# Gated mix of attention and SwiGLU: half of the input turned on TensorE, the last output tiles paced and the feed-forward part added by an identity product

## Chip, cores and metric

The kernel runs on one core of one Trainium2 chip. The metric is the device time of an execution in microseconds. A second number appears beside it, the span of the profiled execution: the time from the profile's first instruction to its end, which is a little shorter than the device time of the same execution. Engine names are those of the profile: PE (TensorE), PEld (its weight loads), DVE (VectorE), ACT (ScalarE), POOL (GpSimd), SP (SyncE).

## What is computed

```python
def _A_ref(x, wqkv, wo):                 # attention, S = 2048, D = 512, H = 32, Dh = 16
    qkv = (x @ wqkv).reshape(B, S, 3, H, Dh).transpose(2, 0, 3, 1, 4)
    q, k, v = qkv[0], qkv[1], qkv[2]
    scores = jnp.einsum("bhqd,bhkd->bhqk", q, k) * (Dh ** -0.5)
    p = softmax(scores, axis=-1)
    o = jnp.einsum("bhqk,bhkd->bhqd", p, v)
    return o.transpose(0, 2, 1, 3).reshape(B, S, D) @ wo

def _B_ref(x, w_gate, w_up, w_down):     # feed-forward, F = 1792
    return (silu(x @ w_gate) * (x @ w_up)) @ w_down

g = sigmoid((x * gate_w).sum(-1, keepdims=True))
out = g * _A_ref(x, wqkv, wo) + (1 - g) * _B_ref(x, w_gate, w_up, w_down)
```

All inputs and the output are bf16. Both halves read the same x (2048 tokens by 512).

## The kernel before

**Tiling.** Queries go in four blocks of 512 (`qb`), heads in eight groups of four (`g`); a pair of the two is a unit, 32 units in all. A unit runs over 16 tiles of 128 keys. For each key tile the scores of four heads are needed, in two pairs: two products on PE write a `s_t` tile of 128 x 1024, and one activation on ACT turns it into `e_t` (exp). Part of the key tiles goes another way: their scores land in `d_t`, and DVE makes the exponential from integer and fp16 arithmetic in `y_t` (with `z_t`, `u_t`, and free parts of `kaug` or `wd_t` as scratch). Value products (`o_ps`) gather both kinds into one bank; the softmax's sums come with them, from a column of ones in `vaug`.

**Order.** The work of PE, DVE and ACT is put in a fixed order when the program is built, by a small planner with a clock for each engine (`Plan`, costs in microseconds). `Pacer` holds side work in chains of pieces with a release and a due slot: the projections of Q, K and V, the gate, the feed-forward products (`gu_chain`, `down_pieces`) and the output products (`fin_pieces`). Where a pair of banks is filled together, `two_banks` lets two products of half height run side by side in the array. `m_tile` hands out three PSUM banks (m0 to m2) in turn; a further pool gives the two score tiles, tag `s`, and one bank holds the value products, tag `o`. `keep_warm` puts products on zeros into PE's queue. The planner also puts value products with zero weights (`o_ps<-xT`) where it sees PE idle.

**The head.** x is needed with its columns on the partitions (`xT`). Nine transposing loads on SP's queue bring it, the first four for tokens 0 to 1023 and the rest for the other half. Behind them on the same queue stand the plain loads of the remaining weights. On ACT's queue stand three small loads: 64 columns each of the K, Q and V weights, for head group 0. DVE copies the first two, spaced out, into `wpad`. PE then makes K of group 0 for all tokens (`k0`, into `kp0`), Q for the first block (`qp0`) and V (`v0`). `largest` takes the greatest magnitude of K per partition, `kneg` is the bound derived from it, `bp0` its product with |Q|, and the last step of DVE folds it into the query `q0[0]`. Then the first scores can go out. `ones_rows` fills rows of `kaug` with ones; groups 1 to 4 on DVE, 5 to 7 on POOL.

**The gate.** g is made as 0.5 (1 + tanh(z/2)), in `gval`, and 1 - g in `omg`, once for all tokens.

**The tail.** The feed-forward result of a block is scaled by `omg` when it leaves PSUM (`down_pieces`, into `bblk`). For the last block, `tail(0)` puts eleven output products ahead of the last value products and `tail(1)` one behind them; `last_mm` adds the products of the last two head groups, and `store` makes gval times PSUM plus `bblk` on DVE, tile by tile, and sends each tile from SP's queue.

Of the kernel before, what the change touches and what calls it, by code (L numbers as in the profile page):

```python
# [9 lines left out]
ALU = mybir.AluOpType  # L10
# [68 lines left out]
def kernel(  # L79
# [89 lines left out]


    xT = big.tile([P, DC, S], BF16, name="xT")
    parts = [(0, 2 * QBW, dc) for dc in range(DC)] + [(2 * QBW, S, dc) for dc in range(DC - 1)]
    parts += [(2 * QBW, 3 * QBW, DC - 1), (3 * QBW, S, DC - 1)]
    for t0, t1, dc in parts:
        nc.sync.dma_start_transpose(out=xT[:, dc, t0:t1], in_=x[t0:t1, dc * P:(dc + 1) * P])
    wqk = big.tile([P, DC, 2 * D], BF16, name="wqk")
    for c0 in (D, 0):

        nc.scalar.dma_start(out=wqk[:, :, c0:c0 + 64],
                            in_=A_wqkv[:, c0:c0 + 64].rearrange("(dc p) c -> p dc c", p=P))  # L180

    rb = big.tile([P, NB, QBW], BF16, name="rb")
    wv = rb[:, :, :]
# [7 lines left out]
    wo_t = big.tile([P, NB, D], BF16, name="wo_t")  # L191

    wo_l = big.tile([P, 2, D], BF16, name="wo_l")
    wd_t = big.tile([P, FC, D], BF16, name="wd_t")

    def late_loads():
        nc.sync.dma_start(out=gw_col[:], in_=gate_w.rearrange("(dc p) -> p dc", p=P))
# [35 lines left out]
    def ones_rows(engine, g):  # L233

        engine.memset(kaug[:, g, :].bitcast(F32), 1.0019378662109375)
    for g in range(1, 4):
        ones_rows(nc.vector, g)
    vaug = big.tile([P, KT, G * 4 * VC + 16], BF16, name="vaug")
    nc.gpsimd.memset(vaug[:, :, G * 4 * VC:], 0.0)

# [23 lines left out]
    ident = const.tile([P, P], BF16, name="ident")  # L264
    nc.gpsimd.memset(ident[:], 1.0)
    nc.gpsimd.affine_select(out=ident[:], in_=ident[:], pattern=[[-1, P]], compare_op=ALU.is_equal,
                            fill=0.0, base=0, channel_multiplier=1)

    kb = const.tile([P, NB], F32, name="kb")
    kneg = const.tile([P, NB, 8], BF16, name="kneg")  # L270
# [108 lines left out]
    def two_banks(n, name, a, b, end):  # L379

        st = {}

        def pc(k):
            v, i = divmod(k, n)

            def f():
                if k == 0:
                    while m_ready(2) is None:
                        stuck()
                    st["a"], st["b"] = m_tile(name + "_a"), m_tile(name + "_b")  # L390
                if k == n:
                    sync(ordered(nc.tensor.nop()), st["half"])
                    spend("R", 0.1 if st["seq"] < plan.seq else 1.5)
                for ps, (w, r), h in ((st["a"], a(i), v), (st["b"], b(i), 1 - v)):
                    rows = slice(64 * h, 64 * h + 64)
                    st["half"] = mm(ps[:, :], lhsT=w[rows, :], rhs=r[rows, :], start=(k == i == 0),
                                    stop=(k == 2 * n - 1), tile_position=(64 * h, 0), skip_group_check=True)
# [195 lines left out]
    def gate_pieces(t0):  # L593
        def f():
            gp = m_tile("glog")
            for t in (t0, t0 + 1):
                for dc in range(DC):
                    mm(gp[:, t:t + 1], lhsT=xT[:, dc, t * P:(t + 1) * P],
                       rhs=gw_col[:, dc:dc + 1], start=(dc == 0), stop=(dc == DC - 1))
            spend("F", 2)  # L600

            def end():
                vec.tensor_copy(out=ge[:, t0:t0 + 2], in_=gp[:, t0:t0 + 2])
                m_free(gp, plan.dve)
            later(0.15, end)
        return [(0.7, f, True)]

    def gate_end():
        act(out=ge[:, :], in_=ge[:, :], func=ACT.Tanh, scale=0.5)
        plan.act += 0.2  # L610

        def end():
            vec.tensor_scalar(out=gval[:, :], in0=ge[:, :], scalar1=1.0, scalar2=0.5, op0=ALU.add, op1=ALU.mult)
            vec.tensor_scalar(out=omg[:, :], in0=ge[:, :], scalar1=-0.5, scalar2=0.5, op0=ALU.mult, op1=ALU.add)
        later(0.4, end, plan.act + 0.2)


    def gu_chain(qb, fc):
# [28 lines left out]
            later(0.6, gated, plan.act + 0.25, (qb, fc))  # L647
        return load, two_banks(DC, "gu", rows("g"), rows("u"), done_gu)

    def down_pieces(qb, tq):  # L650

        def rows(t):
            return lambda fc: (mt[:, fc, t * P:(t + 1) * P], wd_t[:, fc, :])

        def done_down(pa, pb):
            for t, p in ((tq, pa), (tq + 1, pb)):
                later(0.65, lambda t=t, p=p: end(t, p))

        def end(t, p):
            n = qb * TQ + t  # L660
            vec.tensor_scalar(out=bblk[:, t, :], in0=p[:, 0:D], scalar1=omg[:, n:n + 1],
                              scalar2=None, op0=ALU.mult)
            m_free(p, plan.dve)
        return two_banks(FC, "dps", rows(tq), rows(tq + 1), done_down)

# [246 lines left out]
    def store(t, a_ps, base, o_t=None):  # L912
# [3 lines left out]
                                 op0=ALU.mult, op1=ALU.add)  # L916
        nc.sync.dma_start(out=out_f[t * P:(t + 1) * P, :], in_=o_t)

    def fin_pieces(qb, tq):
# [40 lines left out]
    for dc in range(DC):  # L960
# [3 lines left out]
        if dc < DC - 1:  # L964
            keep_warm(2)
# [6 lines left out]
    k0_evict(0)  # L972
    for dc in range(DC):
        if dc < DC - 1:
            for tb in (2, 3):
                k0(dc, tb)
        if dc == 0:
            v0(0)
        elif dc < DC - 1:
            keep_warm(3)  # L980
    ones_rows(vec, 4)
    k0(DC - 1, 2)
    largest(1, kp0[1][:, 0:QBW])
    vec.scalar_tensor_tensor(out=kneg0, in0=bsel0, scalar=kpart0[:, 1:2], in1=kneg1, op0=ALU.mult, op1=ALU.min)
    k0(DC - 1, 3)
    largest(2, kp0[1][:, QBW:2 * QBW])
    vec.scalar_tensor_tensor(out=kneg0, in0=bsel0, scalar=kpart0[:, 2:3], in1=kneg0, op0=ALU.mult, op1=ALU.min)
    k0_evict(1)
    v0(8)
    bp0 = m_tile("bp0")  # L990
# [67 lines left out]
    for qb in range(QB):  # L1058
# [37 lines left out]
    def finish(un):  # L1096
# [6 lines left out]
        if un == UNITS - 2:  # L1103
            here[un] = recip_here(osbs[un])
            spend("F", 1, plan.dve + 0.2)
            for i in range(TQ):
                def part(cs=slice(i * P, (i + 1) * P)):
# [2 lines left out]
                                      op=ALU.mult)  # L1110
                    if cs.stop == QBW:
                        m_free(here[un][0], plan.dve)
                later(1.2, part)

    def close(un):
# [80 lines left out]
            pace.cur = c  # L1196
        pace.credit -= emit_piece(c)

    a_ps = []

    def last_mm(w, on):
        for tq in range(TQ):
            mm(a_ps[tq][:, 0:D], lhsT=on[:, tq * P:(tq + 1) * P], rhs=wo_l[:, w, :], start=False, stop=(w == 1))

    def tail(k):

        if k == 0:
            assert all((QB - 1, b) in normed for b in range(NB - 1))
            a_ps.extend(m_tile("a_l")[:, :] for _ in range(2))
            al = ps_s.tile([P, 2 * QBW], F32, tag="s", name="al")  # L1210
            a_ps.extend([al[:, 0:QBW], al[:, QBW:2 * QBW]])
        todo = [(tq, b) for tq in range(TQ) for b in range(NB - 1)]
        for tq, b in todo[:11] if k == 0 else todo[11:]:
            mm(a_ps[tq][:, 0:D], lhsT=onc[QB - 1][:, b, tq * P:(tq + 1) * P], rhs=wo_t[:, b, :],
               start=(b == 0), stop=False)

    def next_pv():
        flush_act()
        while not pv_list(None):
# [133 lines left out]
    un = UNITS - 1  # L1353
    osb = osbs[un]
    tail(1)
    last_mm(0, osbs[un - 1])
# [47 lines left out]
```

## Time and profile before

| what | us |
|---|---|
| median of 7 runs | 848.31 (847.0 to 848.97) |
| the profiled execution | 847.54 |
| its span | 845.8 |
| first exponential on ACT starts | 18.41 |
| last exponential on ACT ends | 833.94 |
| transposing loads on SP's queue, issue of nine | 0.81 to 13.02 |
| PE's granted clock over the span | 0.994 |

Times within the execution count from the start of the span. A group of the profile names the written and the read tile (out<-in), the shapes, the number of instructions, their busy time and mean, and the idle time of the engine just before them with what ended it. Matmuls overlap in the array: one of 512 columns is shown with about 0.38 us, while a row of them starts every 0.215 us. An engine's idle time costs only where something later waits for it.

### The profile page before, as it was taken

What the parts mean: (1) busy time and instruction counts of PE and PEld (TensorE: products, weight loads), DVE (VectorE), ACT (ScalarE), POOL (GpSimd) and SP (SyncE); (2) the same over time, 40 slices, a digit from 0 to 9 for tenths busy, and PEclk for the clock granted to TensorE, in tenths of its full rate; (3) what the DMA queues carried; (4) which work ended last, traced back from release to release, by engine and by line L of the source; (5) the groups of instructions that cost most, each with busy time, mean ns of one, the idle gap of its engine ahead of it and who ended that gap; (6) DMA issues with size and microseconds to landing.
All of it is one profiled execution on the core that took longest, in us unless ns stands there. A gap on an engine that the chain in (4) does not pass through costs nothing.

```text
span 845.8 us, 16257 instructions
## 1 busy us (share of the span) xinstructions
PE 769.6 (91%) x6078; PEld 263.2 (31%) x6078; DVE 797.2 (94%) x1160; ACT 813.8 (96%) x910; POOL 93.3 (11%) x122
## 2 busy tenths in 40 slices
PE   7999998999889998889899989898999899989996
PEld 3222233332322333222223323223333233233332
DVE  6999998999999999999999899999998999999995
ACT  3999999999999999999999999999999999999994
POOL 5010100010011011011101000101010110110100
PEclk9999999999999999999999999999999999999999
DMA  9432435345454334554443354544532544553331
GB/s 201 130 70 44 89 75 113 69 94 103 95 112 100 65 78 101 104 113 92 96 102 71 78 116 86 110 94 92 106 71 55 112 105 92 109 104 76 74 66 36
DMA packets 101447, 78.23 MB, mean 92 GB/s; under 512 B 77792, under 2 KB 89656, under 8 KB 101368
## 3 DMA queue, kind: packets, MB, share of 16 engines
q0 software_dynamic: 12672, 46.14, 28.7%
q1 hardware_dynamic: 87112, 30.86, 15.4%
q8 instruction: 47, 0.77, 0.4%
q10 hardware_dynamic: 1584, 0.20, 0.2%
q14 instruction: 32, 0.26, 0.1%
HBM read 20.83 MB, written 2.34 MB: 27 GB/s over the span
## 4 chain that ended last, share of the span: by engine, by line
DVE 27%; PE 14%; ACT 8%; issue 3%; DMA 1%; ACTq 0%; DVEq 0%
DVE y_t L166 10%; ACT e_t L160 7%; DVE kaug L166 5%; PE s_t L157 4%; DVE u_t L166 4%; PE o_ps L157 2%; DVE z_t L166 2%; DVE mt L166 2%; DVE gs L166 2%; PE dps_b L157 2%; PE d_t L157 1%; PE dps_a L157 1%; PE gu_b L157 1%; DVE osb L166 1%; ACT th L160 1%
## 5 line engine op out<-in xcount | busy, mean ns | idle before, releaser
L160 ACT ACTIVATE e_t<-s_t 128x1024 bf16<-128x1024 f32 x846 | 792.1, 1106 | 7.7 <-PE s_t L157 5.6
L157 PE MATMUL s_t<-qx,kaug 64*128 64x512 bf16 x1376 | 292.5, 381 | 35.5 <-ACT e_t L160 30.6
L166 DVE TENSOR_SCALAR y_t<-d_t 128x512 uint16<-128x512 f32 x356 | 234.7, 682 | 16.4 <-PE d_t L157 13.7
L157 PEld LDWEIGHTS <-kaug 64*128 64x128 bf16 x2048 | 137.2, 93 | 325.8 <-issue 290.7
L157 PE MATMUL o_ps<-e_t,vaug 128*32 128x512 bf16 x1692 | 160.2, 389 | 2.1 <-DVE osb L166 1.0
L157 PE MATMUL gu_a<-xT,wg 64*128 64x512 bf16 x448 | 136.4, 379 | 0.0
L157 PE MATMUL gu_b<-xT,wu 64*128 64x512 bf16 x448 | 135.0, 378 | 1.2 <-DVE y_t L166 0.9
L157 PE MATMUL d_t<-qx,kaug 64*128 64x512 bf16 x288 | 107.7, 379 | 15.3 <-DVE y_t L166 8.3
L157 PEld LDWEIGHTS <-vaug 128*32 128x32 bf16 (+1 forms) x2148 | 45.9, 93 | 146.8 <-issue 145.5
L772 POOL DMA_DIRECT2D y_t<-u_t x44 | 40.3, 915 | 350.7 <-PE s_t L157 187.8
L772 POOL DMA_DIRECT2D y_t<-kaug x38 | 35.9, 946 | 310.4 <-PE s_t L157 184.5
L157 PE MATMUL dps_b<-wd_t,mt 64*128 64x512 bf16 x224 | 65.0, 375 | 0.3 <-DVE y_t L166 0.2
L157 PE MATMUL dps_a<-wd_t,mt 64*128 64x512 bf16 x224 | 64.9, 376 | 0.0
L166 DVE TENSOR_SCALAR z_t<-y_t 128x2048 uint16<-128x2048 uint16 x89 | 61.5, 691 | 2.1
L166 DVE TENSOR_SCALAR y_t<-y_t 128x2048 uint16<-128x2048 uint16 x89 | 60.9, 684 | 0.8 <-DMA y_t<-u_t 0.4
L166 DVE TENSOR_TENSOR u_t<-u_t 128x2048 f16<-128x2048 f16 x44 | 53.8, 1223 | 1.1
L166 DVE TENSOR_TENSOR u_t<-u_t,z_t 128x2048 f16<-128x2048 f16 x44 | 53.5, 1216 | 0.1
L157 PE MATMUL s_t<-q,kaug 64*128 64x512 bf16 x212 | 44.0, 387 | 7.6 <-ACT e_t L160 7.0
L166 DVE TENSOR_TENSOR kaug<-kaug 128x2048 f16<-128x2048 f16 x39 | 47.7, 1223 | 0.9
L157 PEld LDWEIGHTS <-wg 64*128 64x128 bf16 x448 | 41.5, 94 | 20.7 <-issue 9.0
L166 DVE TENSOR_TENSOR kaug<-kaug,z_t 128x2048 f16<-128x2048 f16 x39 | 47.5, 1217 | 0.1
L157 PEld LDWEIGHTS <-wu 64*128 64x128 bf16 x448 | 42.1, 94 | 15.3 <-issue 0.2
(119 smaller groups left out, 632.2 us busy)
## 6 DMA issues: line engine op xcount, KB each, us to landing
y_t<-u_t POOLq DMA_DIRECT2D x44, 512.0 KB, 4.8
y_t<-kaug POOLq DMA_DIRECT2D x38, 512.0 KB, 5.0
wg<-in_B_w_gate_dram SPq DMA_DIRECT2D x56, 128.0 KB
wu<-in_B_w_up_dram SPq DMA_DIRECT2D x56, 128.0 KB
y_t<-wd_t POOLq DMA_DIRECT2D x6, 512.0 KB, 4.6
on<-osb SPq DMA_DIRECT2D x120, 16.0 KB
rb<-rr SPq DMA_DIRECT2D x15, 128.0 KB
wd_t<-in_B_w_down_dram SPq DMA_DIRECT2D x7, 256.0 KB
```

The source lines that it names most:

```text
L157: return ordered(nc.tensor.matmul(*args, **kw))
L160: ordered(nc.scalar.activation(*args, **kw))
L166: return lambda *a, **kw: ordered(f(*a, **kw))
L772: nc.gpsimd.dma_start(out=ya, in_=ua, accum_op=ALU.add)
```

## The change

Four parts.

1. Only tokens 0 to 1023 of x come by transposing loads. The other 1024 tokens come as two plain loads of 512 KB on ACT's queue, into the still unused tile `wd_t`, one behind the K weights and one behind the Q weights. `turn` multiplies each 128 x 128 block with an identity on PE (four blocks to a bank), and ACT or DVE copies the bank into `xT`. The order of the head is written anew around that; fewer warm products remain, `kp0[1]` is reduced in one step instead of two, and both V products come after the last K product. The identity is made first on POOL, and all `ones_rows` go to POOL.
2. The gate is made as 1/(1 + exp(-z)), with z held within 60; `ge` keeps exp(-z).
3. The last block's feed-forward result is scaled by `ge` instead of `omg`, and added in PSUM by a product with the identity, so that gval times PSUM is the output. Steps on DVE and ACT take turns for this, and their stores go from SP's and ACT's queues.
4. The output products of the last block's first two tiles are a paced chain (`last_pieces`), ready once what they read is made; those of the other two stand, five and five, around the last value products. Where the last unit has one key tile left on ACT's side and a DVE tile ready, the DVE tile goes first.

```diff
-    parts = [(0, 2 * QBW, dc) for dc in range(DC)] + [(2 * QBW, S, dc) for dc in range(DC - 1)]
-    parts += [(2 * QBW, 3 * QBW, DC - 1), (3 * QBW, S, DC - 1)]
-    for t0, t1, dc in parts:
-        nc.sync.dma_start_transpose(out=xT[:, dc, t0:t1], in_=x[t0:t1, dc * P:(dc + 1) * P])
+    for dc in range(DC):
+        nc.sync.dma_start_transpose(out=xT[:, dc, 0:2 * QBW], in_=x[0:2 * QBW, dc * P:(dc + 1) * P])
...
-    for c0 in (D, 0):
+    wd_t = big.tile([P, FC, D], BF16, name="wd_t")
+    for i, c0 in ((0, D), (1, 0)):
...
+        nc.scalar.dma_start(out=wd_t[:, TQ * i:TQ * i + TQ, :],
+                            in_=x[(2 + i) * QBW:(3 + i) * QBW, :].rearrange("(i p) d -> p i d", p=P))
...
-    for g in range(1, 4):
-        ones_rows(nc.vector, g)
...
-    for g in range(5, G):
+    for g in range(1, G):
         ones_rows(nc.gpsimd, g)
...
-                vec.tensor_copy(out=ge[:, t0:t0 + 2], in_=gp[:, t0:t0 + 2])
+                vec.tensor_scalar(out=ge[:, t0:t0 + 2], in0=gp[:, t0:t0 + 2], scalar1=-60.0, scalar2=60.0,
+                                  op0=ALU.max, op1=ALU.min)
...
-        act(out=ge[:, :], in_=ge[:, :], func=ACT.Tanh, scale=0.5)
+        act(out=ge[:, :], in_=ge[:, :], func=ACT.Exp, scale=-1.0)
...
-            vec.tensor_scalar(out=gval[:, :], in0=ge[:, :], scalar1=1.0, scalar2=0.5, op0=ALU.add, op1=ALU.mult)
-            vec.tensor_scalar(out=omg[:, :], in0=ge[:, :], scalar1=-0.5, scalar2=0.5, op0=ALU.mult, op1=ALU.add)
+            vec.tensor_scalar(out=omg[:, :], in0=ge[:, :], scalar1=1.0, scalar2=None, op0=ALU.add)
+            vec.reciprocal(gval[:, :], omg[:, :])
+            vec.tensor_tensor(out=omg[:, :], in0=ge[:, :], in1=gval[:, :], op=ALU.mult)
...
+            share = omg if qb < QB - 1 else ge
+            vec.tensor_scalar(out=bblk[:, t, :], in0=p[:, 0:D], scalar1=share[:, n:n + 1],
                               scalar2=None, op0=ALU.mult)
...
+    def last_rows(t):
+        cs = slice(t * P, (t + 1) * P)
+        return lambda i: ((onc[QB - 1][:, i, cs], wo_t[:, i, :]) if i < NB - 1 else
+                          (osbs[UNITS - 2][:, cs], wo_l[:, 0, :]) if i == NB - 1 else (ident[:, :], bblk[:, t, :]))
+
+    def last_pieces():
+
+        def keep(pa, pb):
+            a_ps.extend([pa, pb])
+        return two_banks(NB + 1, "a_l", last_rows(0), last_rows(1), keep, stop=False)
+
+    def tail(k):
+
+        if k == 0:
+            assert here_done and len(scaled) == TQ
+            for c in list(pace.chains):
+                force(c)
+            al = ps_s.tile([P, 2 * QBW], F32, tag="s", name="al")
+            a_ps.extend([al[:, 0:QBW], al[:, QBW:2 * QBW]])
+        todo = [(tq, i) for tq in (2, 3) for i in range(NB + 1)]
+        for tq, i in todo[:5] if k == 0 else todo[5:]:
+            w, r = last_rows(tq)(i)
+            mm(a_ps[tq][:, 0:D], lhsT=w, rhs=r, start=(i == 0), stop=False)
...
+    def turn(blk, dc):
+        i = len(tps) % 3
+        tps.append((ps_m[1].tile([P, QBW], F32, tag="m1", name="tp") if i == 0 else
+                    ps_m[2].tile([P, QBW], F32, tag="m2", name="tp") if i == 1 else
+                    ps_o.tile([P, QBW], F32, tag="o", name="tp")))
+        tp = tps[-1]
+        for k in range(TQ):
+            mm(tp[:, k * P:(k + 1) * P], lhsT=wd_t[:, TQ * blk + k, dc * P:(dc + 1) * P], rhs=ident[:, :],
+               start=True, stop=True)
+        dst = xT[:, dc, (2 + blk) * QBW:(3 + blk) * QBW]
+        if dc % 2:
+            act(out=dst, in_=tp[:, :], func=ACT.Copy)
+        else:
+            vec.tensor_copy(out=dst, in_=tp[:, :])
...
-    keep_warm(14)
+    keep_warm(10)
+    for dc in range(DC):
+        turn(0, dc)
+    first_half(0)
+    first_half(1)
+    for dc in range(DC):
+        turn(1, dc)
+        if dc == 1:
+            first_half(2)
+        if dc > 1:
+            k0(dc - 2, 2)
+    k0(2, 2)
+    first_half(3)
+    k0(3, 2)
+    for dc in range(DC):
+        k0(dc, 3)
...
+    k0_evict(0)
+    largest(1, kp0[1][:, :])
+    vec.scalar_tensor_tensor(out=kneg0, in0=bsel0, scalar=kpart0[:, 1:2], in1=kneg1, op0=ALU.mult, op1=ALU.min)
...
+    v0(0)
     k0_evict(1)
     v0(8)
...
+            def ripe():
+                return (all((qb, b) in normed for b in range(NB - 1)) and len(scaled) == TQ and here_done)
+            pace.add(last_pieces(), SLOTS - KT // 2, SLOTS, prev, cond=ripe)
...
-        emit_pv(pv_list(None)[0])
+        ns = pv_list(None)
+        if closed == UNITS - 1 and done_a[closed] == hi[closed] - 1 and vready:
+            ns.reverse()
+        emit_pv(ns[0])
...
-    last_mm(1, on_l)
     for tq in range(TQ):
-        store((QB - 1) * TQ + tq, a_ps[tq], bblk[:, tq, :], mt[:, tq, :])
+        mm(a_ps[tq][:, 0:D], lhsT=on_l[:, tq * P:(tq + 1) * P], rhs=wo_l[:, 1, :], start=False, stop=True,
+           skip_group_check=tq < 2)
+    for tq in range(TQ):
+        t = (QB - 1) * TQ + tq
+        if tq % 2 == 0:
+            vec.tensor_scalar(out=mt[:, tq, :], in0=a_ps[tq][:, 0:D], scalar1=gval[:, t:t + 1], scalar2=None, op0=ALU.mult)
+        else:
+            act(out=mt[:, tq, :], in_=a_ps[tq][:, 0:D], func=ACT.Identity, scale=gval[:, t:t + 1])
+        (nc.sync if tq % 2 == 0 else nc.scalar).dma_start(out=out_f[t * P:(t + 1) * P, :], in_=mt[:, tq, :])
```

`first_half(dc)` is the two `k0` products and the `qp0` product of one column block that stood in a loop before.

More of the change, by code (lines that the diff above doesn't have):

```diff
@@ L193 @@
     wo_l = big.tile([P, 2, D], BF16, name="wo_l")
-    wd_t = big.tile([P, FC, D], BF16, name="wd_t")
     def late_loads():
@@ L235, in ones_rows @@
         engine.memset(kaug[:, g, :].bitcast(F32), 1.0019378662109375)
-    for g in range(1, 4):
-        ones_rows(nc.vector, g)
+    ident = const.tile([P, P], BF16, name="ident")
+    nc.gpsimd.memset(ident[:], 1.0)
+    nc.gpsimd.affine_select(out=ident[:], in_=ident[:], pattern=[[-1, P]], compare_op=ALU.is_equal,
+                            fill=0.0, base=0, channel_multiplier=1)
     vaug = big.tile([P, KT, G * 4 * VC + 16], BF16, name="vaug")
@@ L263 @@
         nc.gpsimd.memset(sel_t[32 * j:32 * j + 1, j:j + 1], 1.0)
[L264 to L267, printed above, removed]
     kb = const.tile([P, NB], F32, name="kb")
@@ L377, in sync, with two_banks @@
                           reason="row halves of one bank")
-    def two_banks(n, name, a, b, end):
+    def two_banks(n, name, a, b, end, stop=True):
         st = {}
@@ L396, in f @@
                     st["half"] = mm(ps[:, :], lhsT=w[rows, :], rhs=r[rows, :], start=(k == i == 0),
-                                    stop=(k == 2 * n - 1), tile_position=(64 * h, 0), skip_group_check=True)
+                                    stop=(stop and k == 2 * n - 1), tile_position=(64 * h, 0), skip_group_check=True)
                 spend("R", 1)
@@ L608, in gate_end @@
     def gate_end():
-        act(out=ge[:, :], in_=ge[:, :], func=ACT.Tanh, scale=0.5)
+        act(out=ge[:, :], in_=ge[:, :], func=ACT.Exp, scale=-1.0)
         plan.act += 0.2
         def end():
-            vec.tensor_scalar(out=gval[:, :], in0=ge[:, :], scalar1=1.0, scalar2=0.5, op0=ALU.add, op1=ALU.mult)
-            vec.tensor_scalar(out=omg[:, :], in0=ge[:, :], scalar1=-0.5, scalar2=0.5, op0=ALU.mult, op1=ALU.add)
-        later(0.4, end, plan.act + 0.2)
+            vec.tensor_scalar(out=omg[:, :], in0=ge[:, :], scalar1=1.0, scalar2=None, op0=ALU.add)
+            vec.reciprocal(gval[:, :], omg[:, :])
+            vec.tensor_tensor(out=omg[:, :], in0=ge[:, :], in1=gval[:, :], op=ALU.mult)
+        later(0.5, end, plan.act + 0.2)
     def gu_chain(qb, fc):
@@ L648, in gu_chain @@
         return load, two_banks(DC, "gu", rows("g"), rows("u"), done_gu)
+    scaled = set()
     def down_pieces(qb, tq):
@@ L660, in end @@
             n = qb * TQ + t
-            vec.tensor_scalar(out=bblk[:, t, :], in0=p[:, 0:D], scalar1=omg[:, n:n + 1],
+            share = omg if qb < QB - 1 else ge
+            vec.tensor_scalar(out=bblk[:, t, :], in0=p[:, 0:D], scalar1=share[:, n:n + 1],
                               scalar2=None, op0=ALU.mult)
+            if qb == QB - 1:
+                scaled.add(t)
             m_free(p, plan.dve)
@@ L917, in store @@
         nc.sync.dma_start(out=out_f[t * P:(t + 1) * P, :], in_=o_t)
+    here_done = []
+    a_ps = []
+    def last_rows(t):
[17 more added lines that the diff above has]
+            mm(a_ps[tq][:, 0:D], lhsT=w, rhs=r, start=(i == 0), stop=False)
     def fin_pieces(qb, tq):
@@ L957, in k0_evict, with first_half @@
             bias=onescol[:, 0:1], scale=1.0)
-    keep_warm(14)
-    for dc in range(DC):
+    tps = []
+    def turn(blk, dc):
[12 more added lines that the diff above has]
+            vec.tensor_copy(out=dst, in_=tp[:, :])
+    def first_half(dc):
         for tb in range(2):
@@ L963 @@
         mm(qp0[:, :], lhsT=wpad[0][:, dc, :], rhs=xT[:, dc, 0:QBW], start=(dc == 0), stop=(dc == DC - 1))
-        if dc < DC - 1:
-            keep_warm(2)
+    keep_warm(10)
[14 more added lines that the diff above has]
+        k0(dc, 3)
     largest(0, kp0[0][:, :])
@@ L969 @@
     vec.tensor_scalar(out=kneg1, in0=bsel0, scalar1=kpart0[:, 0:1], scalar2=None, op0=ALU.mult)
+    k0_evict(0)
+    largest(1, kp0[1][:, :])
+    vec.scalar_tensor_tensor(out=kneg0, in0=bsel0, scalar=kpart0[:, 1:2], in1=kneg1, op0=ALU.mult, op1=ALU.min)
     for v in range(2):
         vec.tensor_scalar(out=q0[0][:, v, :], in0=q0r[:, :], scalar1=vsel[:, v:v + 1], scalar2=None, op0=ALU.mult)
[L972 to L987, printed above, removed]
+    v0(0)
     k0_evict(1)
@@ L1112, in part @@
                         m_free(here[un][0], plan.dve)
+                        here_done.append(un)
                 later(1.2, part)
@@ L1197, in put_piece @@
         pace.credit -= emit_piece(c)
[L1199 to L1215, printed above, removed]
     def next_pv():
@@ L1355 @@
     tail(1)
-    last_mm(0, osbs[un - 1])
     dt = m_tile("dt")
```

## The prediction

> **What bounds the kernel now.** I read the page's parts 1 and 5 first, then the timeline of the two ends, the windows of the head and the waits.
>
> ```profile
> PE 769.6 (91%) x6078; PEld 263.2 (31%) x6078; DVE 797.2 (94%) x1160; ACT 813.8 (96%) x910; POOL 93.3 (11%) x122
> ...
> L160 ACT ACTIVATE e_t<-s_t 128x1024 bf16<-128x1024 f32 x846 | 792.1, 1106 | 7.7 <-PE s_t L157 5.6
> ```
>
> ACT, DVE and PE are all nearly full; 846 exponentials fill ACT for 792.1 us and wait 7.7 us in all. So the span splits into three: the head up to the first exponential, a long middle, and the tail after the last one. The timeline of the head (start, duration, engine, what, count, idle before):
>
> ```profile
> 0.81 12.21 SPq L175 DMA_TRANSPOSE xT<-in_A_x_dram  x9
> 5.23 0.26 DVE L230 COPY mt<-wqk 128x256 bf16<-128x256 bf16 x1 [1.31 <-DMA wqk<-in_A_wqkv_dram]
> 14.67 0.10 PEld L157 LDWEIGHTS <-mt 128*128 128x128 bf16 x1 [0.75 <-DMA xT<-in_A_x_dram]
> 15.20 0.38 PE L157 MATMUL kp<-xT,mt 128*128 128x512 bf16 x1 [0.78 <-DVE kpart L166]
> 16.75 0.39 PE L157 MATMUL bp<-aq,mt 128*128 128x512 bf16 x1 [0.24 <-DVE mt L166]
> 17.98 0.39 PE L157 MATMUL s_t<-qx,kaug 64*128 64x512 bf16 x2 [0.84 <-ACT vaug L160]
> 18.41 2.98 ACT L160 ACTIVATE e_t<-s_t 128x1024 bf16<-128x1024 f32 x3 [0.47 <-PE s_t L157]
> ```
>
> The nine transposing loads set the head: the last piece of xT comes at 14.67, the last K product ends about 15.6, and from there the maximum, the bound and the query take 2.8 us to the first exponential at 18.41. Two windows give the rates of the DMA engines, while they transpose and while they load plainly (last column GB/s):
>
> ```profile
> 7.00:8.00 1.00, 1.00 (x7) 0.44 (x5) 0.84 (x2) 0.00 (x0) 1.00 (x2) 1.00 1.23 191
> 17.00:18.00 1.00, 0.16 (x3) 0.11 (x2) 0.83 (x2) 0.94 (x2) 0.00 (x0) 1.00 1.08 372
> ```
>
> The timeline of the tail:
>
> ```profile
> 824.56 9.38 ACT L160 ACTIVATE e_t<-s_t 128x1024 bf16<-128x1024 f32 x10
> 834.31 1.47 PE L157 MATMUL a_l<-wo_t,on 128*128 128x512 bf16 x6
> 835.62 1.24 PE L157 MATMUL al<-wo_t,on 128*128 128x512 bf16 x5
> 836.79 0.40 PE L157 MATMUL o_ps<-y_t,vaug 128*32 128x512 bf16 x4
> 837.24 0.69 DVE L166 CAST osb<-o_ps 128x512 bf16<-128x512 f32 x1 [4.59 <-PE o_ps L157]
> 838.21 0.24 PE L157 MATMUL dt<-sel_t,osb 128*128 128x4 bf16 x4
> 839.61 0.60 PE L157 MATMUL a_l<-wo_l,on_l 128*128 128x512 bf16 x2 [0.40 <-DVE on_l L166]
> 840.83 2.31 SPq L917 DMA_DIRECT2D out_dram<-mt  x4
> 841.38 1.40 DVE L166 SCALAR_TENSOR_TENSOR mt<-al,gval,bblk 128x512 bf16<-128x512 f32 x2
> ```
>
> The last exponential ends at 833.94 and the program at 845.8: 11.9 us in which ACT does nothing. Eleven output products stand ahead of the last value product on PE (834.31 to 836.79), and four scale-and-add steps follow one another on DVE (840.06 to 842.78).
>
> **What the Trainium skill says.** "DMA: Bandwidth & Descriptors", section "Issuing engines are not separate DMA queues": loads started on ScalarE and SyncE run on the same 16 DMA engines and interleave. The trace agrees: the DMA share is 1.06 to 1.37 from 2 to 9 us, and the small query weights, issued on ACT's queue before 1.8 us, are in use only at 5.23. So the plain half doesn't travel free beside the transposing half. "VectorE: DVE Perf Modes", "The three transpose paths": a 128x128 block costs 390 ns on TensorE (into PSUM, a copy follows) and 1309 ns by the DMA crossbar. This case's trace is kinder to the DMA (eight blocks per issue, 1.26 to 1.58 us each), so I use the trace. "TensorE: Matmul & The Clock Gate", Part 1: the clock is halved until about 3.4 us of activity, and again after an idle window of that length. Here the first ten warm matmuls come 0.43 apart, later ones 0.215. "ScalarE: Activation LUTs", "Table sets": exp and tanh share a set, so the gate's Exp needs no table load; the trace has one load, with both functions in use.
>
> **The middle.** The built order of the changed kernel holds the same 846 exponentials, 89 DVE exponential tiles and all products in the same order from the first score to the last twenty, but for the gate (one DVE instruction more, 0.17 us by its neighbours; one exponential changes place with a tanh). I take +0.1.
>
> **The head, step by step.** Removed: five transposing loads, 14 of 24 warm matmuls, four DVE memsets of 0.91, one maximum. The memsets go to POOL, which then runs seven at 0.95 from about 9 to 16 us; the rows are needed much later. Added: two plain loads of 512 KB on ACT's queue, each ahead of a small weight load, 32 products of 128 columns and eight evictions.
> Loads: 1.05 MB transposed at 200 GB/s is 5.2 us, 1.05 MB plain at 370 is 2.8, the three small ones 1.3 (2.9% of a 45 us window): 9.3. The same sum for before is 10.5 + 1.3 = 11.8 from 2.0, so 13.8, and the trace shows 14.67: 0.9 of loss. After: 2.0 + 9.3 + 0.9 = 12.2 for the last piece. That's only 2.5 earlier. I take the last transposed piece at 12.2 and the second plain block, one place ahead of it, at 10.5 (bounds 8.5 and 13).
> On ACT, the V weights' load now waits for the first transposing load's semaphore, and behind it stand the table load (1.28) and ACT's evictions; done near 7.5, before it matters. On DVE, the first eviction is queued behind the copy of the query weights, which now land behind a block, near 7; it holds the fourth turn by a bank until about 8.
> PE from 10.5: two turns (4 products of 0.06 each, from 0.034 for 64 columns and 0.215 for 512) 0.5, three products 0.65, then turns and K products, one held by an eviction (0.69 on DVE, 0.6 on ACT) until 12.65, three products with the last transposed piece to 13.5, five K products to 14.6. That's 1.0 before the old 15.6. But what follows is longer: both V products (2 x 1.1) now stand between the last K product and the bound, and the second maximum covers 1024 columns (1.23 for 0.69). DVE: maxima 13.35 to 14.6 and 14.8 to 16.05, bound 16.4. PE: V to 16.8, bound product to 17.25, query 0.7 to 18.0, score, exponential at 18.5. The wait removed is replaced by V and DVE: head +0.1, bounds -1.4 and +2.
>
> **The tail, step by step.** Two of the four output tiles (20 half-height products, 2.2 us on PE) are now paced into the last exponentials, where PE still waited 1.6 us for ACT and ran idle fillers (16 fewer now). The second of their banks comes free with the DVE scaling that ended at 826.34, so a score goes out about 0.4 late against 0.25 of slack: +0.2 (0 to 0.8), which ACT does not win back.
> After the last exponential (833.94 unshifted): DVE's value tile, ready since 832.65, goes first; five products for tile 2 can start when their bank's exponential ends (833.0), so they end at 834.15; the last value products end at 834.6, against 837.2. Copy 0.69 to 835.3; the other five products lie beside it (to 835.45); sums, reciprocal, broadcast and scaling keep their 1.9 us, to 837.4; the four last products to 837.9. Eviction now scales only, DVE and ACT alternating: DVE 837.3 to 838.0 and 838.7; ACT 837.45 to 838.05, a DMA issue of 0.55, then its second, which in the built order waits for DVE's read of the same tile, 838.75 to 839.35. From the last eviction to the end it was 3.0 (842.78 to 845.8): end 842.35. Tail -3.45 unshifted; bounds -4 and -2.5, since no store of ACT's queue is in the trace.
>
> **Sum.** +0.1 + 0.1 + 0.2 - 3.45 = about -3.1: span 845.8 to 842.7, the profiled run's 847.54 to 844.4. The seven runs' median, 848.31, lies 0.8 above that run; less 3.1 it's 845.2.
>
> **Rivals.**
> The head wins too (0.16): both blocks at 8.5, the last transposed piece near 10.5. For it: the small loads on ACT's queue got through quickly once begun; against it: DMA share over 1 all through. First exponential 17.2: 843.8.
> The tail's gain is eaten (0.14): the paced products hold scores back by a microsecond and ACT's store lands late. For it: a slot of six half products and a score takes 1.07 against ACT's 0.91; against it: two score buffers and fillers that were idle. 847.2, no change within what can be told.
> Slower (0.12): the plain block starves. The three weight loads of 448 KB on SP's queue used to stand behind nine transposing loads and now stand behind four; with 1.34 MB at 370 they take 3.7. If they and all transposing loads pass ahead of the second block, it lands at 2.0 + 5.2 + 1.3 + 2.8 + 3.7 + 0.9 = 15.9, and PE waits there: first exponential 23.9, +5.4 for the head, and PE's clock may fall in the pause. Total 850.7. It decides from about 15.3 for that landing (tail 3.1 plus 1.7). Against it: interleaving gives ACT's queue a share from 2 us on.
> The forecast itself has 0.58.
>
> **Range and chances.** The forecast's own range is 844.0 to 846.4. Reaching over the first two rivals: 843.2 to 848.4. Two tenths of a per cent (1.7 us) is about what this measurement can tell from no change: faster 0.74, same 0.15, slower 0.11.
>
> **What would show it.** Right: first exponential between 17.5 and 19.3; the last K product ending before 15 and the bound product directly behind V; the last value product within 0.7 of the last exponential; two output steps each on DVE and ACT; 8.4 from the last exponential to the end. Wrong: a PE wait for wd_t past 12, matmuls of the head 0.43 apart after 6 us, gaps of ACT over 0.5 among the last ten exponentials, or an ACT store that takes over 3.5 to the end.

## The result, and the profile after

The changed kernel is slower: 854.3 us in the median of 15 runs (851.31 to 856.59) against 848.66 for the kernel before beside it, a ratio of 1.0059 with a 95% interval of 1.0046 to 1.0073, that is about 5.0 us. The forecast was 845.2 with a range up to 848.4. The profiled execution took 855.08 us with a span of 853.4.

Split as the prediction split it, at the first exponential's start and the last one's end:

| stretch of the span, us | before | after | difference |
|---|---|---|---|
| head, to the first exponential | 18.41 | 26.81 | +8.40 |
| middle | 815.53 | 818.07 | +2.54 |
| tail, from the last exponential's end | 11.86 | 8.52 | -3.34 |

The tail gave what was forecast (-3.45). The head, forecast at +0.1, took it back more than twice over. First the page's parts 1 and 5 of the kernel after (busy time, share of span, instructions; then busy time and mean ns of one, and idle time before):

```profile
PE 770.9 (90%) x6092; PEld 265.5 (31%) x6092; DVE 802.6 (94%) x1157; ACT 818.4 (96%) x916; POOL 97.0 (11%) x126
...
L160 ACT ACTIVATE e_t<-s_t 128x1024 bf16<-128x1024 f32 x846 | 792.9, 1103 | 9.3 <-PE s_t L157 7.7
```

Nothing is to be seen here: the exponentials fill 792.9 us where it was 792.1, with 9.3 of waiting where it was 7.7. A loss before the first exponential doesn't appear in this group. The timeline of the head does show it (start, duration, engine, what, count, idle before and who ended it):

```profile
7.54 1.81 POOL L480 MEMSET qx<- 128x2048 bf16 x1
7.90 7.78 DVE L230 COPY mt<-wqk 128x256 bf16<-128x256 bf16 x1 [1.46 <-DMA wqk<-in_A_wqkv_dram]
8.04 7.64 DVE L166 CAST xT<-tp 128x512 bf16<-128x512 f32 x2
9.29 6.29 POOL L235 MEMSET kaug<- 128x1024 f32 x7
15.76 0.58 PE L157 MATMUL tp<-ident,wd_t 128*128 128x128 bf16 x4 [8.53 <-DVE xT L166]
16.14 1.06 PE L157 MATMUL kp<-xT,mt 128*128 128x512 bf16 x2
22.08 1.24 PE L157 MATMUL kp<-xT,mt 128*128 128x512 bf16 x5
25.15 0.39 PE L157 MATMUL bp<-aq,mt 128*128 128x512 bf16 x1
26.81 1.02 ACT L160 ACTIVATE e_t<-s_t 128x1024 bf16<-128x1024 f32 x1 [0.40 <-PE s_t L157]
```

DVE's copy of the Q weights into `wpad` starts at 7.90, as soon as its data is there, and lasts 7.78 us. The same copy took 0.26 before. It ends at 15.68; POOL's last memset ends at 15.58. (The K weights' copy, 0.66 before, takes 2.92 here, from 3.52 to 6.44, beside other memsets of POOL; no product waits for it.) The evictions of the turned banks stand behind it on DVE (8.04, 7.64 long), the fourth turn waits for a bank, and PE stands still for 8.53 us. Then two products come 0.43 apart, not 0.215. The windows tell why (length of the window; PE, PEld, DVE, ACT, POOL busy; granted clock; DMA share; GB/s):

```profile
8.00:9.00 1.00, 0.00 (x0) 0.00 (x0) 1.00 (x3) 0.99 (x2) 1.00 (x1) 1.00 1.15 249
10.00:11.00 1.00, 0.00 (x0) 0.00 (x0) 1.00 (x3) 0.00 (x0) 1.00 (x2) 0.50 0.88 93
18.00:19.00 1.00, 1.00 (x6) 0.45 (x4) 0.00 (x0) 0.00 (x0) 0.00 (x0) 0.50 1.01 351
20.00:21.00 1.00, 1.00 (x13) 0.65 (x12) 0.30 (x2) 0.39 (x1) 0.00 (x0) 1.00 0.08 16
```

DVE counts as fully busy from 8 on, but with one instruction that doesn't advance. PE idles, its clock falls to half and stays there until about 19.8, though work came back at 15.76. After 6.38 no product of the head waits for a load.

The tail, in the timeline of the kernel after:

```profile
837.33 7.56 ACT L160 ACTIVATE e_t<-s_t 128x1024 bf16<-128x1024 f32 x8
845.18 0.40 PE L157 MATMUL o_ps<-e_t,vaug 128*32 128x512 bf16 x4
845.64 0.69 DVE L166 CAST osb<-o_ps 128x512 bf16<-128x512 f32 x1 [2.04 <-PE o_ps L157]
848.00 0.39 PE L157 MATMUL a_l_a<-wo_l,on_l 128*128 128x512 bf16 x1 [0.40 <-DVE on_l L166]
848.46 0.74 DVE L166 TENSOR_SCALAR mt<-a_l_a,gval 128x512 bf16<-128x512 f32 x1
848.65 0.69 ACT L160 ACTIVATE mt<-a_l_b,gval 128x512 bf16<-128x512 f32 x1 [3.76 <-PE a_l_b L157]
849.89 0.69 ACT L160 ACTIVATE mt<-al,gval 128x512 bf16<-128x512 f32 x1 [0.56 <-DVE mt L166]
```

The last exponential ends at 844.88, the last value products 0.70 later at 845.58 (it was 837.19 - 833.94 = 3.25 before), and the last eviction at 850.58.

The middle's +2.54 is one step: numbered in order, the exponentials of both profiles run 7.9 to 8.7 us apart up to number 320 and 10.1 to 11.0 apart after number 360. At 350.85 of the profile after, DVE waits 1.47 for an accumulating transfer into `y_t`. Whether that belongs to the change is tested below.

### The profile page after: what moved, and what is told of

It is laid out like the page before. It is cut to its first block, busy times and chain, and to the rows that moved or that the text cites. A ratio compares the mean times of both kernels' runs of the same rounds, so it can differ in the third digit from the quotient of the medians.

```text
span 853.4 us, 16298 instructions
## 1 busy us (share of the span) xinstructions
PE 770.9 (90%) x6092; PEld 265.5 (31%) x6092; DVE 802.6 (94%) x1157; ACT 818.4 (96%) x916; POOL 97.0 (11%) x126
## 5 line engine op out<-in xcount | busy, mean ns | idle before, releaser
L160 ACT ACTIVATE e_t<-s_t 128x1024 bf16<-128x1024 f32 x846 | 792.9, 1103 | 9.3 <-PE s_t L157 7.7
```

What stands on the lines that cost most here:

```text
L160: ordered(nc.scalar.activation(*args, **kw))
```

## The experiments

**Theory.** POOL's memsets and DVE's one-input bf16 copy exclude each other. The change moved four memsets to POOL's queue, so the copy, which took 0.26 before, falls into a row of eight (that of `qx` and seven of `kaug`, one behind the other without a gap) and waits for the whole row; the idle PE then loses its clock. The Trainium skill has the exclusion, in "SBUF — State Buffer", section "Who interferes with whom": DVE and GpSimd share one pair of SBUF ports; copies, casts and scalar steps of DVE that use both its ports compete for it, whoever comes first has it for the whole instruction, and the other stands. A two-input step doesn't compete with a POOL instruction that only writes. The runs below show the exclusion and what escapes it (7.78 us as a copy, 0.34 with two inputs); ports they don't show. **Rival A**: the Q weights and x come late because of the queues. **Rival B**: any work of DVE is slowed beside POOL. **Rival C**: the tail's edits cost time in the middle.

**The copy in another form.** In the changed kernel, both copies into `wpad` become a maximum of the weights with themselves, which has two inputs and gives the same values:

```diff
-        nc.vector.tensor_copy(
-            out=wpad[i][:, :, :].rearrange(...)[:, :, :, 1:1 + DH],
-            in_=wqk[:, :, i * D:i * D + 64].rearrange("p dc (j c) -> p dc j c", c=DH))
+        w64 = wqk[:, :, i * D:i * D + 64].rearrange("p dc (j c) -> p dc j c", c=DH)
+        nc.vector.tensor_tensor(
+            out=wpad[i][:, :, :].rearrange(...)[:, :, :, 1:1 + DH],
+            in0=w64, in1=w64, op=ALU.max)
```

> The changed kernel, with the two copies of K and Q weights into wpad written as a maximum of wqk with itself (two inputs, same result); POOL's memsets and all loads stay. Theory (POOL's memsets shut out DVE's one-input copy of the Q weights, 7.8 us in place of 0.3): the two-input form isn't shut out, the second copy takes under 0.6 and ends near 8.5, first exponential between 17.5 and 19.5 in place of 26.81, time about 8 below the changed kernel: 845 to 847. Rival A (the Q weights and x come late through the DMA queues): copy as long as before, first exponential near 26.8, 854. Rival B (DVE is slowed by POOL in any form): two-input form blocked too, 854.

Measured: 847.26 (ratio to before 0.9985, 0.9969 to 1.0). From the timeline of this run:

```profile
7.44 1.81 POOL L481 MEMSET qx<- 128x2048 bf16 x1
8.15 0.34 DVE L231 TENSOR_TENSOR mt<-wqk 128x256 bf16<-128x256 bf16 x1 [3.93 <-DMA wqk<-in_A_wqkv_dram]
8.36 1.28 DVE L166 CAST xT<-tp 128x512 bf16<-128x512 f32 x2
9.18 6.29 POOL L236 MEMSET kaug<- 128x1024 f32 x7
```

POOL's row is where it was, and the copy takes 0.34 in the midst of it; so do the casts out of PSUM, 0.69 each as always. Rivals A and B fall as causes of the long copy. But the first exponential is at 21.19, not between 17.5 and 19.5, and the time is 0.3 above what was expected: a second cause of 2 to 3 us is left.

**POOL held back.** The copies stay as they are; POOL's memsets of `q1`, `qx[0]` and the seven groups of `kaug` wait until the second copy is done:

```diff
-    nc.gpsimd.memset(q1[:], 0.0)
-    nc.gpsimd.memset(qx[0][:], 0.0)
+    after_copy(nc.gpsimd.memset(q1[:], 0.0))
+    after_copy(nc.gpsimd.memset(qx[0][:], 0.0))
     for g in range(1, G):
-        ones_rows(nc.gpsimd, g)
+        after_copy(ones_rows(nc.gpsimd, g))
```

> The changed kernel, with POOL's memsets of q1, qx and the seven groups of kaug held back until DVE's second weight copy is done; copy form and loads stay. Theory: the copy takes 0.3 once its data is there, near 7.5, first exponential 17.5 to 19.5 if POOL's later memsets shut out no other step of DVE; as the maxima's small copy and the query's steps then fall beside the memsets (about 7.5 to 15.5), one of them may be late by up to 1. Time 845 to 848. Rival A (queues): 854 and first exponential near 26.8.

Measured: 848.27 (0.9995, 0.9982 to 1.0008), first exponential 21.20. DVE's part of its timeline:

```profile
3.15 2.41 DVE L230 COPY mt<-wqk 128x256 bf16<-128x256 bf16 x1 [0.22 <-DMA wqk<-in_A_wqkv_dram]
8.08 0.26 DVE L230 COPY mt<-wqk 128x256 bf16<-128x256 bf16 x1 [2.52 <-DMA wqk<-in_A_wqkv_dram]
17.71 0.81 DVE L166 TENSOR_SCALAR mt<-mt,kpart 128x128 bf16<-128x128 bf16 x1
```

With POOL silent the one-input copy is 0.26 again. The other two lines are the same exclusion at other places: the K weights' copy stands under an earlier memset, and at 17.71 the scalar step of the bound lasts 0.81 until 18.52, when the held-back row (12.18 to 18.47) is over. The head is as long as in the run before, again later than the expected 17.5 to 19.5, and PE's clock is at half in both (8.1 to 14.9 here, 8.3 to 15.1 there): the second cause seems common to both.

**Four memsets back on DVE**, three between and behind the weight copies and one later, so that POOL keeps groups 5 to 7:

```diff
+    for g in range(1, 4):
+        ones_rows(nc.vector, g)
...
-    for g in range(1, G):
+    for g in range(5, G):
         ones_rows(nc.gpsimd, g)
...
+    ones_rows(vec, 4)
     k0(2, 2)
```

> The changed kernel, with the memsets of groups 1 to 4 back on DVE at the places they had, POOL keeping groups 5 to 7 and the zeros of qx. Theory: POOL is done with its row of memsets some 3.8 earlier, so near 11.8, and the copy of the Q weights ends there in place of 15.68; first exponential near 22 to 23, time 849 to 851. If the wait is one instruction's and not a row's, the copy ends near 8 and the time is 845 to 847. Rival A (queues): 854.

Measured: 848.74 (1.0004, 0.9993 to 1.0015), first exponential 23.09.

```profile
7.98 4.16 DVE L230 COPY mt<-wqk 128x256 bf16<-128x256 bf16 x1 [1.53 <-DMA wqk<-in_A_wqkv_dram]
9.30 2.74 POOL L235 MEMSET kaug<- 128x1024 f32 x3
```

The row ends 3.54 sooner than in the changed kernel, and so does the copy: at 12.14, again 0.1 behind the last memset (12.04). It waits for the row, not for one memset of 0.95. The first exponential is close to what was expected (22 to 23), the time 0.3 below.

**The tail alone**: the changed gate and tail with the head of before, that is with its nine transposing loads, its memsets on DVE and its order of products. The identity alone is still made first on POOL; the two weight copies end at 6.44 and 6.52 for that (3.92 and 5.48 before), and the first K product starts 0.06 later.

> The changed kernel's gate and tail with the head of before (nine transposing loads, memsets, order of products). Theory (all the loss is the head's, the tail's gain is whole): first exponential at 18.4, from the last exponential to the end 8.5 in place of 11.9, time 3.3 below before: 845.2. Rival C (the tail's edits cost 2 to 3 us in the middle): 847 to 848.

Measured: 845.4 (0.996, 0.9945 to 0.9975), first exponential 18.58. The gain is whole without the head's part; this version is faster than both kernels. Rival C, which asked for 847 to 848, falls.

**The memsets alone.** The kernel before, with groups 1 to 4 of `ones_rows` on POOL too and no other edit:

> The kernel before with one part of the change alone: all seven memsets of kaug on POOL, nothing else. Theory (a row of POOL's memsets shuts out DVE's one-input bf16 steps): POOL's row now ends near 15.6; the step mt<-mt,kpart on DVE (0.39 in before, at 11.57) lasts until then, about 4 us, and the query's steps, both last maxima and the bound stand behind it: first exponential 20.5 to 22 in place of 18.41, time 2 to 3.5 above before. If the loss needs the new loads: no change, 18.4.

Measured: 849.21 (1.0019, 1.0007 to 1.0032), first exponential 20.21.

```profile
5.22 0.26 DVE L230 COPY mt<-wqk 128x256 bf16<-128x256 bf16 x1 [1.32 <-DMA wqk<-in_A_wqkv_dram]
9.17 6.30 POOL L235 MEMSET kaug<- 128x1024 f32 x7
10.86 4.66 DVE L166 TENSOR_SCALAR mt<-mt,kpart 128x128 bf16<-128x128 bf16 x1
```

Here the weights come early and their copy is free (0.26 at 5.22), but the next one-input step falls into the row: 4.66 in place of 0.39, ending 0.05 after the row. So this part of the change costs time with the old loads as well, by another instruction. The size is below what was expected (2 to 3.5), 0.6 to 2.7 us by the interval and 1.8 in the head, since the maximum behind that step on DVE has to wait for a K product of late x in any case: it starts at 15.83 here, and at 14.45 in the profile of before. The other 0.4 of the head is PE's clock, at half from 17.7 to 27.9 in this execution, after a pause of 2.1 us: the bound product takes 0.61 in place of 0.39, and from the first score to the first exponential it is 0.64 in place of 0.43. By exponential 40 that stretch has cost another 2.2, and the execution ran 3.1 above its own median. It doesn't come in every execution: the mean granted clock is 0.987 to 0.992 in four of the fourteen, which took 850.96 to 853.68 us, and 0.995 to 0.999 in the others, which took 847.83 to 850.16.

**PE kept at work.** The version with the copies as maxima, with more products on zeros:

```diff
-    keep_warm(10)
+    keep_warm(16)
     for dc in range(DC):
+        if dc == DC - 1:
+            for _ in range(4):
+                mm(qp0[:, :], lhsT=idle[:, 0:P], rhs=idle[:, :], start=True, stop=True)
         turn(0, dc)
```

> The run with the copies as maxima, and PE kept at work: 16 warm products in place of 10, and four more (into the bank that Q of the first block takes next) ahead of the fourth turned column. Theory (the 2.8 us that stayed there, 21.19 against 18.41, are PE's clock, granted at half from 8.4 to 15): no slice of the head under full clock after 6, last K product near 14.6 in place of 17.7, first exponential 18 to 19.3; the step mt<-mt,kpart falls before the end of POOL's memsets at 15.5 and lasts until then. Time 844.5 to 846. Rival (x's second block or the last transposed piece sets the end): first exponential stays near 21, time 847.

Measured: 846.17 (0.9978, 0.996 to 0.9995), 0.2 above what was expected, and the first exponential as expected, at 18.64:

```profile
18.64 3.07 ACT L160 ACTIVATE e_t<-s_t 128x1024 bf16<-128x1024 f32 x3 [0.40 <-PE s_t L157]
```

Two windows at the same place, first of the run without these products (the copies as maxima):

```profile
14.00:15.00 1.00, 1.00 (x7) 0.64 (x6) 0.00 (x0) 0.00 (x0) 1.00 (x2) 0.50 1.07 371
```

and with them:

```profile
14.00:15.00 1.00, 1.00 (x7) 0.41 (x5) 1.00 (x1) 0.90 (x2) 1.00 (x2) 1.00 1.08 373
```

Both show PE fully busy, at half and at full clock. Without the products PE paused from 5.35 to 7.26 and from 8.10 to 9.10, and its clock was down from about 8.3 to 15.1. The second cause is the clock, and not a late x. The 2.55 us between the two heads (21.19, 18.64) are those of one execution each; in the medians less is seen (0.9978 against 0.9985, with intervals that overlap), and the mean granted clock differs from execution to execution in both versions (0.989 to 0.999 here, 0.991 to 0.997 there). "TensorE: Matmul & The Clock Gate", Part 1, of the Trainium skill has the fall after an idle window of some 3.4 us; here it came 2.9 us after the last product on zeros, with 0.84 us of turning products in between, so this run did not escape it by staying under 3.4 us with each single pause.

**More out of the head.** The version with PE kept at work, with two memsets on DVE between the weight copies and the last maximum in two steps:

```diff
+    for g in range(1, 3):
+        ones_rows(nc.vector, g)
...
-    largest(1, kp0[1][:, :])
+    largest(1, kp0[1][:, 0:QBW])
     vec.scalar_tensor_tensor(out=kneg0, in0=bsel0, scalar=kpart0[:, 1:2], in1=kneg1, op0=ALU.mult, op1=ALU.min)
+    largest(2, kp0[1][:, QBW:2 * QBW])
+    vec.scalar_tensor_tensor(out=kneg0, in0=bsel0, scalar=kpart0[:, 2:3], in1=kneg0, op0=ALU.mult, op1=ALU.min)
```

> The run before this with two memsets of kaug on DVE between the weight copies (POOL's row ends near 13.7), and the last maximum in two steps of 512 columns. Theory: mt<-mt,kpart is short again, the bound ends 0.5 to 1 sooner, first exponential 17 to 18, time 843.5 to 845, below both kernels and 0.5 to 1.5 below the tail alone. Rival (no room left in the head): first exponential over 18.4 and the time that of the tail alone, 845.4, or above.

Measured: 845.98 (0.9973, 0.9964 to 0.9983), first exponential 19.55. The expectation of 17 to 18 was wrong and the rival right: x's second column was waited for until 10.88 (10.42 in the run before), and the split made the bound longer, since all K products were done when the first maximum began (two maxima of 0.68 with two steps of 0.35, in place of 1.22 and 0.35). PE's clock falls in this profile too, behind the first exponential (at half from 20.5 to 27.3). The new head, free of the long copy and of the early fall of the clock, isn't shorter than the old one.

**The wait kept, the clock saved**: the changed kernel with its copies and memsets, with 14 products on zeros at first and 38 ahead of the fourth turn.

> The changed kernel with its copies and memsets as they are, 14 warm products in place of 10 and 38 more ahead of the fourth turned column, so that PE works through the wait. Theory: the copy of the Q weights still ends near 15.7, but PE keeps its full clock, and the head shortens by half of the 3.6 us that ran at half clock: first exponential near 25.0 in place of 26.81. Rival (clock doesn't matter, evictions and loads set the pace): 26.8.

Measured: one execution of 850.29, first exponential 25.07:

```profile
7.59 8.10 DVE L230 COPY mt<-wqk 128x256 bf16<-128x256 bf16 x1 [1.15 <-DMA wqk<-in_A_wqkv_dram]
25.07 1.94 ACT L160 ACTIVATE e_t<-s_t 128x1024 bf16<-128x1024 f32 x2 [0.40 <-PE s_t L157]
```

and one of the windows during the wait:

```profile
12.00:13.00 1.00, 0.95 (x6) 0.43 (x5) 1.00 (x3) 0.00 (x0) 1.00 (x3) 1.00 1.08 196
```

The copy lasts 8.10 and ends at 15.69, with PE at full clock throughout. That splits the head's +8.40: the clock has 26.81 - 25.07 = 1.74, the wait 25.07 - 18.64 = 6.43 (against the run with PE kept at work, which differs in the copies' form and the number of products on zeros), and 18.64 - 18.41 = 0.23 is left for the new head itself. Each part is a difference of two single executions. The changed kernel's own two profiles differ by 0.36 at this point (26.81, and 26.45 below), so the 0.23 can't be told from nothing; and the products on zeros hold the fourth turn until 15.98 here, 15.76 in the changed kernel, so the clock may have up to 0.2 more and the wait as much less. The clock's part has a second witness: of the sixteen executions of the changed kernel with a granted clock on record, four have a mean of 0.996 to 1.0, too high for a stretch of 10 us at half, which alone takes 0.006; their median is 852.6, that of the other twelve 854.6.

**The changed kernel again**, for the middle:

> The changed kernel once more, unedited. Theory: the copy of the Q weights again ends with POOL's row of memsets near 15.6, first exponential near 26.8, time 853 to 854 (4.5 to 5.5 above before); the 2.5 us that its first profile lost in the middle (one step of 2.7 after 352, at an accumulating transfer into y_t) are that execution's own and stay away here, so the middle is 815 to 817 long. Rival (the change lengthens the middle): 818 again, with the step at the same exponential.

Measured: 853.59 (1.0057, 1.0035 to 1.0079), first exponential 26.45, tail 8.51, and the middle 817.14. The copy lasted 8.06 and ended at 15.68. The step of 2.7 isn't there; one of 2.0 stands elsewhere, between exponentials 500 and 600. The middle of the other profiles was 814.76 to 816.93 long, in no order of the edits, and 818.44 in that of the memsets alone; in the profiles of 816.93 and 818.44 PE's clock is down at the beginning of the middle. So 817.14 doesn't show the change to be free there, nor at fault. Head and tail sum to 8.40 - 3.34 = 5.06 in the first profile and to 8.04 - 3.35 = 4.69 in this one, beside the 3.9 to 6.2 of the interval: they account for the loss without the middle, and a cost of up to a microsecond there is not excluded.

**The tail without turns.** The tail alone, with all four last scalings on DVE and all stores on SP's queue:

```diff
-        if tq % 2 == 0:
-            vec.tensor_scalar(...)
-        else:
-            act(out=mt[:, tq, :], in_=a_ps[tq][:, 0:D], func=ACT.Identity, scale=gval[:, t:t + 1])
-        (nc.sync if tq % 2 == 0 else nc.scalar).dma_start(...)
+        vec.tensor_scalar(...)
+        nc.sync.dma_start(...)
```

> The tail-only run with the four last scalings all on DVE and the four stores all on SP's queue; the paced output products and the identity products stay. Theory (of the tail's 3.4 us most come from output products done before the last exponential, the turns of DVE and ACT bring the rest): four scalings at 0.70 end 2.8 after the first one starts, 0.6 to 0.7 later than in turns, so 9.1 from the last exponential to the end in place of 8.5, and 846.0. Rival (the turns bring most of it): over 10, and 847 or more.

Measured: 845.07 (0.9969, 0.9958 to 0.998), from the last exponential to the end 9.35, against 8.52 in the changed kernel and 8.84 in the tail-only run's profile. So the turns of DVE and ACT bring 0.5 to 0.8 of the tail's 3.3. The rest, 2.5, is what the last value products come sooner (0.70 after the last exponential, as in the changed kernel, in place of 3.25), now that the output products no longer stand between; what the order of the last two key tiles has in it was not tried. In the medians these two versions can't be told apart.

## Why the prediction was wrong

**The step that failed** is this sentence of the head: "The memsets go to POOL, which then runs seven at 0.95 from about 9 to 16 us; the rows are needed much later." Times and need were right (9.29 to 15.58). The step asked only who waits for the memsets' result, and priced their place on POOL at nothing. Who is shut out while they run was not asked. So the next term of the sum, the first eviction, which "holds the fourth turn by a bank until about 8", was wrong by 7.8 us: the fourth turn started at 15.76. That cost 6.43 us of waiting and 1.74 of clock.

The trace of before had it, in three lines of the head's timeline that I had passed over:

```profile
3.26 0.66 DVE L230 COPY mt<-wqk 128x256 bf16<-128x256 bf16 x1 [0.33 <-DMA wqk<-in_A_wqkv_dram]
...
9.17 2.74 POOL L235 MEMSET kaug<- 128x1024 f32 x3
11.57 0.39 DVE L166 TENSOR_SCALAR mt<-mt,kpart 128x128 bf16<-128x128 bf16 x1
```

The prediction showed the second weight copy, 0.26, not its twin of the same shape, 0.66. And the scalar step of 0.39 (0.26 with POOL silent, as in the changed kernel at 23.32) ends at 11.96, just after POOL's memsets at 11.91. A group whose single instructions differ by a factor of 2.5 was the sign.

**The other steps of the head.** "On DVE, the first eviction is queued behind the copy of the query weights": that was seen, and this queue is where the loss was passed on to PE; for the copy's own length the prediction took one that nothing had held up. With the copy and the clock mended, the sum's end comes out: first exponential 18.64 where 18.5 was forecast, the last K product ending at 15.14 (forecast 14.6). That is in part luck. The sum has PE wait for the second plain block until 10.5; in the run with PE kept at work PE waits for the second transposed column until 10.42, a wait that the sum doesn't have, and takes up the second block at 11.06 without one. The reading that the wait removed is replaced by DVE's two maxima and the V products was right.

**The warm products** (the products on zeros). The prediction counted 14 of 24 as taken away; the traces have 26 before and 10 after, so 16 went. It costed that at nothing in the forecast, with a fall of PE's clock only in the rival with the late block. Even without the shut-out copy it costs 2.55 us in the head of the profiled execution (21.19 against 18.64). That is the second error of the head.

**The rivals.** The slower rival (850.7) had the right sign, stage and consequence for the clock, but a wrong cause: PE waited for a bank behind DVE, not for a plain block; the first was in use at 6.38, the second at 18.70 without a wait. Of the signs named for a wrong forecast, products 0.43 apart after 6 us was the one that came.

**The tail**: right step by step. Last value products 0.70 after the last exponential (forecast 0.7); two scalings each on DVE and ACT, ACT's second waiting for DVE's; the end 8.52 after the last exponential (forecast 8.4). Of the slip of 0.2 before the tail the profile shows nothing: eight exponentials stand without a gap at the end. **The gate**: no effect seen; it is in the tail-only run too, whose 845.4 is near the forecast for the whole.

The best version by its ratio is thus the tail and gate of the change with the old head: 845.4, about 3.4 below before, 2.1 to 4.7 by the interval. The intervals of the run without turns and of the two with PE kept at work overlap with it.

## What to carry to other kernels

When work is moved to POOL, look not only at who waits for it but at which one-input bf16 steps of DVE from SBUF to SBUF fall into the same stretch: each of them may stand until POOL's row is over, and everything queued behind it on DVE stands too. Beside memsets, which only write, such a step can be written with two inputs (0.34 us here in place of 0.26), or POOL's work put where DVE has none of them. And read each instruction of a group apart: a copy that takes 0.66 once and 0.26 the next time may have waited for something that no wait in the profile names.

## What was not expected of the hardware

The section of the Trainium skill named above speaks of a lock for one instruction. Here a copy of 0.26 us stood through a row of eight memsets, for 7.78, 8.10 and 8.06 us in three executions, 4.16 with four memsets, and a scalar step stood 4.66 through the greater part of seven; each ended within 0.12 us of the row's last one. Between two memsets of such a row DVE never got in.

The profile counts the standing as busy time of DVE and names no releaser for it; the waits show it only one engine on, as PE waiting 8.53 us for DVE's `xT`.

PE's clock came back slowly: in the run with the copies as maxima PE worked from 9.10 without a gap, and full clock returned at 15.1; in the changed kernel work came back at 15.76 and full clock at about 19.8. In the twelve traces of this document every stretch at half clock that lies whole inside the span is 3.41, 6.83 or 10.24 us long, that is one, two or three times 3.41; the seven in the head or just behind it are of 6.83 or 10.24.
